# Top-k attention and an MLP-mixer on one core: which score tiles are masked by an adding DMA, the order of the first loads, and a newly fitted instruction order

## The chip, the cores and the metric

The kernel runs on one core of a Trainium2 chip. The metric is the device time of one execution in microseconds (us). Three runs of the kernel before gave 759.48, 761.50 and 761.62 us; the median is 761.5 us.

## The reference

The reference is attention over 8 batches of 8 heads, 576 positions and a head size of 64, in which each row keeps only its 32 largest scores, followed by a token and channel mixing MLP on the joined heads. In short:

```python
scores = scale * q @ k.T                      # (8, 8, 576, 576)
kth    = 32nd largest of each row
attn   = softmax(where(scores >= kth, scores, -1e9))
x      = join_heads(attn @ v)                 # (8, 576, 512)
h      = relu(x.T @ w_tok1) @ w_tok2          # 576 -> 256 -> 576
u      = x + h.T
out    = u + relu(u @ w_ch1) @ w_ch2          # 512 -> 1536 -> 512
```

## The kernel before

The work goes by pairs of heads, 32 pairs in all (`pair_ops(p)`), four pairs to a batch. A pair has five groups of score tiles: groups 0 to 3 hold one tile of 128 rows of each of the two heads, and group 4 is a single tile that holds the last 64 rows of both heads. So a pair has nine tiles of 128 rows by 576 columns, and the kernel has 288.

Each tile passes through all engines in turn. TensorE transposes q and k (L426) and makes the scores in PSUM (`products`, L488, for the groups of two; `last`, L494, for the single tile). ScalarE copies them into an `Sb` buffer (L578). VectorE takes the eight largest of each of seven segments (L588) and narrows the 56 candidates in five dependent steps (L593 to L600); this gives an upper bound for the 32nd largest. GpSimd shifts and scales the scores by that bound into integers (L632). ScalarE counts by the sign how many lie above (L635), GpSimd appends eight dummy values made from the count (L638), and VectorE takes the eight largest of the remaining integers (L643), among which the 32nd largest of the row stands at a known place. GpSimd turns it into a threshold (L651) and writes a byte mask `U` (L666): a row's dropped scores get a huge negative number, the kept ones none.

The masked exponentials are then made in one of two ways:

- **Recomputed.** TensorE puts the mask into PSUM as a product with a scaled identity (`lower`, L510, for a pair of tiles; `again`, L500 and L504, for a single one), adds the scores once more on top of it, and ScalarE takes the exponential from PSUM into a `Pm` buffer (L676 for a pair, L682 for a single tile). There are two `Pm` buffers.
- **Added by DMA.** ScalarE takes the exponential of the unmasked scores early, from `Sb` into a `Pe` buffer (L625). When the mask is there, GpSimd issues a DMA that adds `U` to `Pe` as 16-bit integers (L686). There are four `Pe` buffers. TensorE has no part in it.

The set `ADDED` says which groups (p, g) go the second way. In both ways SyncE then issues a transposing DMA into `PT` (single tiles: `PTl`), L690, TensorE multiplies by v (`pv`, L706), and VectorE divides by the row sums (`norm`, L715 and L716). The last groups of pair 31 go a third way (`direct`, L529 to L564), in which VectorE masks and TensorE transposes.

After the fourth pair of a batch, `mlp_ops(b)` adds the MLP of that batch: L751 to L834 on TensorE, its evictions on ScalarE (L763, L791, L811, L842). The last batch's MLP is cut up (`token`, `channel`): nine of its twelve column blocks are begun with half of the sum (L941, called L964), saved by ScalarE (L966), and finished by an addition on VectorE (L989). A self-check (`judge`, L1074 to L1117, and the flag, L1126 and L1129) runs on VectorE near the end; if it fails, the whole result is recomputed by slower code.

No engine's order is written by hand. `Plan` is a list scheduler that runs while the kernel is built: each operation has an engine, a duration, dependencies, buffers that it takes from pools (`Sb` 11, `Pm` 2, `Pe` 4, `PT` 6, PSUM 4), and a due time made of its tile's number times `T` plus an entry of the table `DUE`. Among the operations that could start at about the same time, the one with the earliest due time goes first. Every engine, and every DMA queue, then works strictly in that order. In idle time of TensorE between two fixed points, the scheduler also puts small filler matmuls (L370), six at a time.

At the start, the first pair's loads are issued by hand-set priorities: k's halves on ScalarE's and SyncE's queues (L455), q in pieces on SyncE's (L449: the first 128 rows of both heads, then the other three blocks; L460: the last 64 rows), k's last rows on ScalarE's (L467). Before that, VectorE builds constants (L313, L314) and clears the unused part of the load buffers (L318).

## Time and profile before

One execution was profiled. Its own time was 763.86 us, and the span from its first to its last instruction 762.1 us; the median of the three runs shown above is 761.5 us.

| what | value |
|---|---|
| profiled execution, its own time | 763.86 us |
| span in the profile | 762.1 us |
| TensorE busy | 728.7 us (96%) |
| VectorE busy | 718.8 us (94%) |
| ScalarE busy | 684.4 us (90%) |
| GpSimd busy | 586.4 us (77%) |
| mean granted TensorE clock | 0.995 |

Engines are named PE (TensorE matmuls), PEld (its weight loads), DVE (VectorE), ACT (ScalarE), POOL (GpSimd) and SP (SyncE); a name with q is that engine's queue of instructions, which waits and issues DMAs. A busy PE is not a PE at its peak, because matmuls overlap and their ends are modelled. In the list of instructions over time a row gives start, duration, engine, line, operation, tiles, shapes and count, and in brackets how long the engine stood idle before it and what ended that.

### The profile page before, as it was taken

To read this page: it belongs to the slowest core of one execution; us is meant where nothing else is said; L and a number is where in the kernel's file an instruction comes from. 1 tells how busy PE (TensorE), PEld (TensorE's weight loads), DVE (VectorE), ACT (ScalarE), POOL (GpSimd) and SP (SyncE) were. 2 spreads that over 40 slices of the span, in tenths; PEclk is the share of its full clock that TensorE was granted. 3 is DMA by queue.
4 is the path that set the end of the run, shared out by engine and by line. 5 is a ranking of instruction groups with operands and counts; after the bars stand their busy time and mean duration, and the time that the engine had idled before them with its cause. 6 is when DMAs were issued, how large, how long until landed. Compare 5 with 4: busy or idle time off the path is not lost.

```text
span 762.1 us, 21660 instructions
## 1 busy us (share of the span) xinstructions
PE 728.7 (96%) x6517; PEld 508.1 (67%) x6517; DVE 718.8 (94%) x4466; ACT 684.4 (90%) x1350; POOL 586.4 (77%) x1053
## 2 busy tenths in 40 slices
PE   6989999999999999999999999999989999999997
PEld 4766777677657776667666765667747776677663
DVE  7997999999999999999999999999999999999861
ACT  5868999899889998999989998899989999999852
POOL 3696989987877878778787878877789888988600
PEclk9998999999999999999999999999999999999999
DMA  5598999967887678767787656887759988876602
GB/s 124 91 157 145 142 158 180 170 124 118 148 147 140 125 115 163 151 119 128 118 157 151 121 108 123 168 162 126 139 115 166 152 135 160 137 125 88 123 18 72
DMA packets 293658, 101.15 MB, mean 133 GB/s; under 512 B 269856, under 2 KB 290208, under 8 KB 293536
## 3 DMA queue, kind: packets, MB, share of 16 engines
q1 hardware_dynamic: 279152, 83.86, 59.0%
q0 software_dynamic: 13632, 15.57, 14.6%
q8 instruction: 52, 0.85, 0.4%
q14 instruction: 70, 0.57, 0.2%
q10 hardware_dynamic: 752, 0.30, 0.1%
HBM read 35.85 MB, written 9.44 MB: 59 GB/s over the span
## 4 chain that ended last, share of the span: by engine, by line
DVE 41%; PE 39%; ACT 8%; POOL 6%; issue 3%; DMA 2%; ACTq 0%; DVEq 0%; POOLq 0%; SPq 0%
DVE cd L588 16%; PE bank L488 13%; DVE tlo L643 12%; PE bank L830 4%; PE bank L805 4%; PE bank L706 3%; ACT sign L635 3%; DVE cd L598 3%; PE bank L510 2%; DVE cd L594 2%; POOL U L666 2%; DVE Xb L716 2%; DVE thi L600 2%; PE bank L494 2%; POOL Sb L632 2%
## 5 line engine op out<-in xcount | busy, mean ns | idle before, releaser
L588 DVE MAX8 cd<-Sb 128x8 f32<-128x82 f32 (+1 forms) x2016 | 386.3, 231 | 2.0 <-ACT Sb L578 1.9
L488 PE MATMUL bank<-kT,qT 64*128 64x288 f32 x1712 | 242.2, 422 | 6.2 <-ACT kT L433 3.8
L635 ACT ACTIVATE sign<-Sb,half 128x576 bf16<-128x576 int32 x283 | 226.9, 802 | 20.4 <-POOL Sb L632 12.9
L666 POOL TENSOR_SCALAR U<-Sb,nt 128x576 uint8<-128x576 int32 x283 | 212.3, 750 | 25.7
L632 POOL TENSOR_SCALAR Sb<-Sb,ng 128x576 int32<-128x576 f32 x283 | 217.2, 779 | 13.2 <-ACT Pe L625 6.0
L643 DVE MAX8 tlo<-Sb 128x8 f32<-128x584 uint32 x283 | 214.0, 756 | 8.8 <-POOL Sb L638 8.0
L488 PEld LDWEIGHTS bank<-kT,qT 64*128 64x128 f32 x1712 | 153.9, 188 | 72.7 <-issue 21.7
L578 ACT COPY Sb<-bank 128x576 f32<-128x576 f32 x288 | 167.5, 685 | 10.3 <-PE bank L488 7.5
L676 ACT ACTIVATE Pm<-bank 128x576 bf16<-128x576 f32 x172 | 105.4, 664 | 7.3 <-PE bank L488 7.1
L805 PE MATMUL bank<-UT,wc1b 128*128 128x288 bf16 x672 | 90.2, 286 | 3.6 <-ACT UT L791 1.5
L830 PE MATMUL bank<-wc2b,H 128*128 128x512 bf16 x372 | 88.1, 379 | 0.4 <-ACT H L811 0.4
L805 PEld LDWEIGHTS <-wc1b 128*128 128x128 bf16 x672 | 64.6, 98 | 27.1 <-issue 9.3
L830 PEld LDWEIGHTS <-H 128*128 128x128 bf16 x372 | 34.6, 98 | 40.8 <-issue 6.0
L635 ACT ACTIVATION_READ_ACCUMULATOR sign<-Sb,half 128x1 f32 x283 | 61.7, 218 | 0.0
L651 POOL TENSOR_SCALAR nt<-tlo 128x2 f32<-128x2 f32 (+1 forms) x157 | 35.8, 228 | 32.3 <-DVE tlo L643 12.8
L510 PE MATMUL bank<-U,identN 128*128 128x288 bf16 x344 | 58.1, 288 | 1.2 <-POOL U L666 0.5
L600 DVE MAX8 thi<-cd 128x8 f32<-128x56 f32 x288 | 58.3, 202 | 0.0
L686 POOL DMA_DIRECT2D Pe<-U x40 | 50.4, 1259 | 6.7 <-POOL U L666 4.5
L811 ACT ACTIVATE H<-bank 128x576 bf16<-128x576 f32 x84 | 54.4, 676 | 0.0
L638 POOL TENSOR_TENSOR Sb<-kdum,cnt 128x16 int32<-128x16 int32 (+1 forms) x157 | 36.7, 235 | 21.5 <-ACT sign L635 17.7
L598 DVE MATCH_REPLACE8 cd<-m,cd 128x35 f32<-128x35 f32 x288 | 52.5, 182 | 0.0
L596 DVE MAX8 m<-cd 128x8 f32<-128x35 f32 x288 | 51.9, 180 | 0.1
(140 smaller groups left out, 1067.9 us busy)
## 6 DMA issues: line engine op xcount, KB each, us to landing
Pe<-U POOLq DMA_DIRECT2D x40, 288.0 KB, 4.7
vL<-in_v_dram SPq DMA_DIRECT2D x32, 256.0 KB, 3.0
kL<-in_k_dram SPq DMA_DIRECT2D x63, 128.0 KB, 3.1
qL<-in_q_dram SPq DMA_DIRECT2D x62, 128.0 KB, 2.9
out_dram<-ob SPq DMA_DIRECT2D x15, 512.0 KB, 3.0
wc1b<-in_moe_w_ch_dram POOLq DMA_DIRECT2D x4, 384.0 KB, 5.1
wc2b<-in_moe_w_ch_dram POOLq DMA_DIRECT2D x4, 384.0 KB, 6.5
PT<-Pm SPq DMA_TRANSPOSE x86, 3.9
```

Source lines behind the costliest of these rows:

```text
L488: nc.tensor.matmul(out=halves(s.t)[:, h, :], lhsT=qT.t[rows(h), g * P : (g + 1) * P], rhs=kT.t[rows(h), i * HS : (i + 1) * HS], start=star ...
L578: ev.append(plan.add("ACT", 0.535, t + DUE["cp"] + 0.01 * i, lambda n=n, i=i, s1=s1, Sb=Sb: nc.scalar.copy(out=Sb.t[:, 0:n, i * HS : (i + ...
L588: ss.append(plan.add("DVE", 0.146, t + DUE["seg"] + 1.0 * h, lambda a=a, h=h, cd=cd, Sb=Sb: nc.vector.max(cd.t[:, a, :], Sb.t[:, h, bounds ...
L598: a4 = plan.add("DVE", 0.157, tr_, lambda m8=m8, cd=cd: nc.vector.match_replace(cd.t[:, :, 0:5], m8.t[:, 1, :], cd.t[:, :, 0:5], NEG), [a3 ...
L600: a5 = plan.add("DVE", 0.12, tr_, lambda i=i, cd=cd: nc.vector.max(thi[:, at(i) - 7 : at(i) + 1], cd.t[:, :, :]), [a4] + tops[-1:], use=[cd])
L632: xo.append(plan.add("POOL", 0.725, t + DUE["x"] + 0.9 * h, lambda k=at(i) - lo, h=h, Sb=Sb, X=X, nb=nb: nc.gpsimd.tensor_scalar(out=X.t[: ...
L635: sgn.append(plan.add("ACT", 0.77, t + DUE["sg"] + 0.8 * h, lambda i=i, h=h, X=X: nc.scalar.activation(out=sign[:, :], in_=X.t[:, h, 0:S]. ...
L643: mxs.append(plan.add("DVE", 0.67, t + DUE["mx"] + 1.2 * h, lambda i=i, h=h, X=X: nc.vector.max(tlo[:, at(i) - 7 : at(i) + 1], X.t[:, h, : ...
L666: us.append(plan.add("POOL", 0.84, t + DUE["u"] + 0.01 * h, lambda h=h, k=at(i0 + h) - lo, nt=nt, U=U, X=X: nc.gpsimd.tensor_scalar(out=by ...
L676: oe.append(plan.add("ACT", 0.54, t + DUE["ex"], lambda i=i, s2=s2, Pm=Pm: nc.scalar.activation(out=Pm.t[:, :, i * HS : (i + 1) * HS], in_ ...
L805: nc.tensor.matmul(out=o[:, i, :], lhsT=wc1b[:, cc, fc * P : (fc + 1) * P], rhs=UT.t[:, cc, i * HS : (i + 1) * HS], start=(cc == 0), stop= ...
L830: nc.tensor.matmul(out=po, lhsT=H2.t[:, fc, cs], rhs=wc2b[:, fc, :], start=(fc == 0), stop=False)
```

## The change

`ADDED` held 40 groups, all of them pairs of tiles: group 1 of pairs 0 to 30 and group 3 of pairs 22 to 30. It now holds 61: group 1 and the single tile, group 4, of pairs 5 to 30, and group 3 of pairs 22 to 30. So 26 single tiles move from recomputing to the adding DMA, and five pairs of tiles (group 1 of pairs 0 to 4) move the other way. On the engines that makes 26 times fewer L500 with L504 and L682 and five times more L510 with L488 and L676; 26 more early exponentials and adding DMAs of one tile, and five fewer of two.

In the first pair, the first 128 rows of q of both heads now come with one DMA, the buffers' unused part is cleared first of all on VectorE, 13 small matmuls (`warm`) go ahead of the first transposes and three behind the first of q, and q's transposes are cut into three pieces (block 0; blocks 1 to 3; the last rows) with a copy for each. Groups 1 to 3 then need only the second piece.

`T` and the whole table `DUE` have new numbers, and a few durations that the scheduler plans with changed by up to 0.04 us. The core of the diff:

```diff
-ADDED = {(p, 1) for p in range(31)} | {(p, 3) for p in range(22, 31)}
+ADDED = {(p, g) for p in range(5, 31) for g in (1, 4)} | {(p, 3) for p in range(22, 31)}
...
-T = 1.71610
+T = 1.64060
 DUE = dict(
...
-    mm=-231.700, mx=-97.622, ng=6.727, nm=1.107, nt=-276.380, pv=-124.790, re=-244.310, rnd=-75.253,
+    mm=-290.100, mx=-210.470, ng=-108.730, nm=-6.943, nt=-334.450, pv=-139.730, re=-276.010,
...
+    for t in qLs + kLs:
+        nc.vector.memset(t[:, 4, :, :], 0.0)
     make_identity(nc, identF[:, :])
...
-    for t in qLs + kLs:
-        nc.vector.memset(t[:, 4, :, :], 0.0)
...
+    def warm(s, n):
+        a = 1024 * s + 1024 - 184
+        for _ in range(n):
+            nc.tensor.matmul(out=bank[:, a : a + 184], lhsT=identB[:, :], rhs=identF[:, :].bitcast(bf16)[:, 0:184],
+                             start=True, stop=True)
...
+            def first_q():
+                nc.sync.dma_start(
+                    out=qL.t[:, 0, :, :],
+                    in_=q[b, h0 : h0 + 2, 0:SM, :].rearrange("h (p t) d -> p t h d", t=4)[:, 0, :, :])
...
+            def turn_first():
+                turn(pq, qL, (0,))()
+                warm(3, 3)
+
+            o0 = plan.add("PE", 0.7, -98.0, turn_first, [q0], acq=[pq, qT], use=[qL], lat=-0.3)
             k1 = plan.add("PE", 0.43, -97.0, turn(pk, kL, (3, 4)), [k0, lc], use=[pk, kT, kL])
-            o1 = plan.add("PE", 0.86, -96.0, turn(pq, qL, (1, 2, 3, 4)), [o0, q1, q2], use=[pq, qT, qL])
+            o1 = plan.add("PE", 0.65, -97.5, turn(pq, qL, (1, 2, 3)), [o0, q1], use=[pq, qT, qL])
+            o2 = plan.add("PE", 0.22, -96.0, turn(pq, qL, (4,)), [o1, q2], use=[pq, qT, qL])
...
-                    [eq[g > 0]] + ek[: i + 1 if n == 2 else 2], acq=[s1[i]] + ([Sb] if i == 0 else []), use=[qT, kT, Sb], mode=3 if n == 2 else 0)
+                    [eq[0 if g == 0 else 1 if g < 4 else 2]] + ek[: i + 1 if n == 2 else 2], acq=[s1[i]] + ([Sb] if i == 0 else []), use=[qT, kT, Sb], mode=3 if n == 2 else 0)
...
+    warm(3, 13)
     for i, o in enumerate(order):
```

Where the new order matters to the steps of the prediction, it reads as follows. Line numbers of the changed kernel are 3 higher around the transposes and 12 higher from the scores on (L488 is now L500, L635 is L647, L676 is L688, L966 is L978).

The first place is TensorE at the very start, in the first pair; `kL_77` and `qL_75` are its load buffers, `qT_85` and `kT_88` the transposed ones. Before:

```order
L426 MATMUL bank<-identF,kL_77 128x128 x3
L426 MATMUL bank<-identF,qL_75 128x128
L426 MATMUL bank<-identF,kL_77 128x128 x2
L488 MATMUL bank<-kT_88,qT_85 128x288 x4
L426 MATMUL bank<-identF,qL_75 128x128 x4
L488 MATMUL bank<-kT_88,qT_85 128x288 x12
L494 MATMUL bank<-kT_88,qT_85 128x288 x2
```

Now, behind thirteen small matmuls, three transposes of k, the first of q and two more of the small matmuls:

```order
L366 LDWEIGHTS identB
L366 MATMUL bank<-identF,identB 128x184
L429 MATMUL bank<-identF,qL_75 128x128 x3
L429 MATMUL bank<-identF,kL_77 128x128 x2
L429 MATMUL bank<-identF,qL_75 128x128
L500 MATMUL bank<-kT_88,qT_85 128x288 x16
L506 MATMUL bank<-kT_88,qT_85 128x288 x2
```

Before, the first four score matmuls stood ahead of the transposes of q's other blocks; now all transposes, that of q's last rows too, stand ahead of the first score matmul.

The second place is ScalarE around the fourth pair's start, where the exponentials of the first pair's groups are taken; `Pm_124` and `Pm_125` are the two `Pm` buffers, and the single tile is the row of 128x576 out of the bank. Before:

```order
L676 ACTIVATE Pm_125<-bank 128x2x288 x2
L578 COPY Sb_93<-bank 128x2x288 x2
L635 ACTIVATE sign,cnt<-Sb_97,half 128x576
L676 ACTIVATE Pm_124<-bank 128x2x288 x2
L578 COPY Sb_94<-bank 128x576
L635 ACTIVATE sign,cnt<-Sb_97,half 128x576
L635 ACTIVATE sign,cnt<-Sb_98,half 128x576 x2
L682 ACTIVATE Pm_125<-bank 128x576
L430 ACTIVATE qT_85<-bank 128x640
L433 COPY kT_88<-bank 128x576
```

Now:

```order
L688 ACTIVATE Pm_124<-bank 128x2x288
L590 COPY Sb_93<-bank 128x2x288 x2
L688 ACTIVATE Pm_124<-bank 128x2x288
L647 ACTIVATE sign,cnt<-Sb_97,half 128x576
L688 ACTIVATE Pm_125<-bank 128x2x288 x2
L590 COPY Sb_94<-bank 128x576
L694 ACTIVATE Pm_124<-bank 128x576
L433 ACTIVATE qT_85<-bank 128x640
L436 COPY kT_88<-bank 128x576
```

The first pair fills `Pm` five times now, where it filled it four times. Between the last exponential into the buffer that the single tile needs and the single tile's own, there stood nine instructions before (three copies, four signs, two exponentials); now there are four (a sign, two exponentials, a copy).

The third place is ScalarE near the end, where the saved halves of the last batch (L966, now L978) and the last masked tiles are copied; `PT` rows are the transposed tiles of the last pair. Before:

```order
L919 CAST UT_142<-bank 128x576
L905 ACTIVATE H_140<-bank 128x2x128
L564 COPY PT_134<-bank 128x640
L676 ACTIVATE Pm_125<-bank 128x2x288 x2
L919 CAST UT_142<-bank 128x576
L564 COPY PT_134<-bank 128x640
L966 COPY Sb_93<-bank 128x576 x2
L966 COPY Sb_91<-bank 128x576 x2
L564 COPY PT_130<-bank 128x640
L676 ACTIVATE Pm_124<-bank 128x2x288 x2
L564 COPY PT_130<-bank 128x640
L966 COPY Sb_96<-bank 128x576 x2
```

Now:

```order
L541 ACTIVATE Sb_97<-Sb_99 128x2x576
L978 COPY Sb_91<-bank 128x576 x2
L978 COPY Sb_94<-bank 128x576 x2
L978 COPY Sb_100<-bank 128x576 x2
L978 COPY Sb_98<-bank 128x576 x2
L550 ACTIVATE sign,cnt<-Sb_99,half 128x576 x2
L688 ACTIVATE Pm_124<-bank 128x2x288 x2
L978 COPY Sb_95<-bank 128x576
L550 ACTIVATE sign,cnt<-Sb_101,half 128x576
L576 COPY PT_135<-bank 128x640 x2
L688 ACTIVATE Pm_125<-bank 128x2x288 x2
L576 COPY PT_131<-bank 128x640 x2
```

The saved halves, and so the matmuls that make them, stood between and behind the copies of the last pair's transposed tiles; now all nine stand ahead of them, the first eight even ahead of the signs of those tiles. On VectorE the self-check (L1074 on), which stood between the last masked tile and the last additions, now stands behind the last addition.

More of the change, by code (lines that the diff above doesn't have):

```diff
@@ L361 @@
             moe_w_ch2[3 * i * P : (3 * i + 3) * P, :].rearrange("(j p) c -> p j c", p=P)))
+    def warm(s, n):
[3 more added lines that the diff above has]
+                             start=True, stop=True)
     def filler(s, k):
-        a = 1024 * s + 1024 - 184
         def f():
             if k is not None:
+                a = 1024 * s + 1024 - 184
                 nc.tensor.matmul(out=bank[:, a : a + 1], lhsT=identF[:, :], rhs=thi[:, k : k + 1], start=True, stop=True)
-            for _ in range(6):
-                nc.tensor.matmul(out=bank[:, a : a + 184], lhsT=identB[:, :], rhs=identF[:, :].bitcast(bf16)[:, 0:184],
-                                 start=True, stop=True)
+            warm(s, 6)
         return f
@@ L790, in mlp_ops @@
             o = plan.add("PE", 0.98, due(0.98), f, [h1] + wl["w2"], acq=[pb] + ([UT] if cc == 0 else []), use=[X, H1, pb])
-            ut.append(plan.add("ACT", 0.54, due(0.0) + 1, lambda cc=cc, pb=pb: nc.scalar.copy(
+            ut.append(plan.add("ACT", 0.58, due(0.0) + 1, lambda cc=cc, pb=pb: nc.scalar.copy(
                 out=UT.t[:, cc, 0:S].rearrange("p (a b) -> p a b", a=2), in_=halves(pb.t)), [o],
```

38 lines of the change are left out of this document (18 added, 20 removed).

## The prediction

> **What bounds the kernel now.** I began with the busy time of each engine by stages, cut where the character of the kernel changes: until the loads of weights end, the long middle, the end of VectorE's searches, the tail. The columns are the length, then busy time of PE, PEld, DVE, ACT and POOL, then clock, DMA share and GB/s.
>
> ```profile
> 8.63:50.00 41.37, 37.82 (x328) 28.97 (x327) 41.09 (x300) 31.43 (x61) 24.97 (x47) 1.00 0.69 124
> 50.00:100.00 50.00, 44.30 (x416) 33.90 (x415) 44.04 (x280) 42.01 (x86) 41.06 (x73) 0.93 0.97 145
> 100.00:600.00 500.00, 488.39 (x4370) 337.78 (x4369) 494.71 (x3132) 474.18 (x942) 411.27 (x743) 1.00 0.77 140
> 600.00:702.80 102.80, 101.49 (x932) 72.33 (x931) 101.34 (x648) 100.99 (x200) 89.98 (x158) 1.00 0.77 127
> 702.80:721.00 18.20, 17.77 (x128) 10.32 (x126) 16.80 (x42) 15.90 (x32) 14.80 (x25) 1.00 0.72 136
> 721.00:762.10 41.10, 34.83 (x344) 22.52 (x341) 16.77 (x41) 17.64 (x32) 0.00 (x0) 0.99 0.19 50
> ```
>
> From 8.6 to 702.8 us VectorE stands still for 0.28 + 5.96 + 5.29 + 1.46 = 13.0 us only, and the change neither adds nor takes an instruction of it. Whatever is taken from TensorE there can be worth 13.0 us at most. After 721 us VectorE is half idle and TensorE carries the chain. Next the waits, to see who made VectorE wait (total, times, longest).
>
> ```profile
> DVE tlo L643 <- POOL Sb L638: 8.0, 10, 4.6
> ...
> DVE rds L715 <- PE bank L706: 6.5, 8, 2.5
> ...
> PE bank L368 <- ACT qT L430: 4.8, 2, 3.9
> ...
> PE bank L488 <- ACT kT L433: 3.8, 5, 1.4
> ...
> ACT Pm L682 <- DMA PT<-Pm: 3.0, 2, 2.7
> ```
>
> One event makes 4.6 of the 8.0. I followed it through the chain of waits and the list over time.
>
> ```profile
> 48.72 7.98 DMA PT<-Pm
> ```
>
> ```profile
> 56.78 0.65 ACT L682 ACTIVATE Pm<-bank 128x576 bf16<-128x576 f32 x1 [2.65 <-DMA PT<-Pm]
> ```
>
> ```profile
> 59.53 4.21 PE L488 MATMUL bank<-kT,qT 64*128 64x288 f32 x16
> ...
> 64.71 2.21 PE L488 MATMUL bank<-kT,qT 64*128 64x288 f32 x16
> ```
>
> ```profile
> 66.49 0.77 DVE L643 MAX8 tlo<-Sb 128x8 f32<-128x584 uint32 x1 [4.62 <-POOL Sb L638]
> ```
>
> A transposing DMA took 7.98 us, where its kind's median is 3.9 (below), while the DMA engines were 97% busy with weights, adding DMAs and loads. ScalarE stood 2.65 us for the `Pm` buffer that it held, the fourth pair's q and k were copied late, TensorE idled 3.9 us, then ran sixteen matmuls in 4.21 us that later took 2.21, and VectorE lost 4.62 us.
>
> **TensorE's work.** In the tail the two ways of masking lie bare on TensorE's queue: a single tile's (L500 to the start of the next line) and a pair's.
>
> ```profile
> 714.54 0.41 PE L500 MATMUL bank<-U,identN 128*128 128x288 bf16 x2
> ...
> 714.78 1.13 PE L504 MATMUL bank<-kT,qT 128*128 128x288 f32 x4
> ...
> 715.75 0.65 PE L898 MATMUL bank<-w2b,H 128*128 128x288 bf16 x4
> ...
> 717.46 0.65 PE L510 MATMUL bank<-U,identN 128*128 128x288 bf16 x4
> ...
> 719.21 0.66 PE L898 MATMUL bank<-w2b,H 128*128 128x288 bf16 x4
> ```
>
> A single costs 715.75 - 714.54 = 1.21 us, a pair 719.21 - 717.46 = 1.75 us. So TensorE loses 26 x 1.21 = 31.5 us and gains 5 x 1.75 = 8.8 us: 22.7 us less. From 100 us on VectorE is the one that is always busy, so nearly all of this turns into idle time of TensorE. What it can bring is in the waits that TensorE caused: the 6.5 us of L715, less two that lie in the tail,
>
> ```profile
> 724.25 0.22 DVE L715 RECIPROCAL rds<-bank 128x10 f32<-128x10 f32 x1 [2.54 <-PE bank L706]
> ...
> 732.43 0.20 DVE L715 RECIPROCAL rds<-bank 128x6 f32<-128x6 f32 x1 [2.15 <-PE bank L706]
> ```
>
> so 1.8 us, and a share of the 3.4 us that L643 has besides its one event. I take **-2 us**; the ends are 0 (nothing but smoothing) and -6.8 (all idle time after 100 us).
>
> **ScalarE and GpSimd.**
>
> ```profile
> L676 ACT ACTIVATE Pm<-bank 128x576 bf16<-128x576 f32 x172 | 105.4, 664 | 7.3 <-PE bank L488 7.1
> ...
> L686 POOL DMA_DIRECT2D Pe<-U x40 | 50.4, 1259 | 6.7 <-POOL U L666 4.5 <-POOL nt L651 1.0 <-POOL ng L609 0.5
> L625 ACT ACTIVATE Pe<-Sb 128x1152 bf16<-128x1152 f32 x40 | 46.8, 1180 | 0.0
> ...
> L682 ACT ACTIVATE Pm<-bank 128x576 bf16<-128x576 f32 x31 | 20.7, 668 | 5.7 <-DMA PT<-Pm 3.0 <-PE bank L504 2.5
> ...
> L336 POOL DMA_DIRECT2D w1b<-in_moe_w_tok_dram x3 | 1.7, 569 | 0.1
> ...
> L529 ACT ACTIVATE Sb<-Sb 128x576 bf16<-128x576 f32 x1 | 0.7, 679 | 0.0
> ```
>
> ScalarE's exponential of one tile is 668 ns from PSUM and 679 from SBUF: 26 x 0.011 = 0.3 us, and the five pairs cost 2 x 664 - 1180 = 148 ns each, 0.7 us; nothing, hidden in its idle time (25.8 us between 100 and 600). GpSimd issues 26 more DMAs of one tile and five fewer of two. The trace has no issue of one tile; the bounds are 569 ns (the small weights) and 1259 ns (two tiles). By the upper, nearer in kind, that is (26 - 5) x 1.26 = 26 us, at least 26 x 0.57 - 6.3 = 8.5. GpSimd has 88.7 us idle between 100 and 600 and behind each issue waits only its own next mask: nothing on the path.
>
> ```profile
> Pe<-U POOLq DMA_DIRECT2D x40, 288.0 KB, 4.7
> ...
> PT<-Pm SPq DMA_TRANSPOSE x86, 3.9
> qL<-in_q_dram SPq DMA_DIRECT2D x64, 16.0 KB, 2.4
> ```
>
> The adding DMA puts up to 4.7 us between a single tile's mask and its transposing DMA, where 1.21 + 0.67 us stood. Single tiles are the pair's last, so `pv` and the norm come some 3 us later. That holds buffers, not VectorE: the norm is due by priority alone, and nothing waits for it until the batch's MLP. SyncE's queue does stand behind such a wait, with the loads of later pairs, which are issued well ahead. Zero, at worst a wait like the 2.65 above now and then.
>
> **The first 100 us.** Without adding DMAs in the first five pairs, five of 288 KB leave the stage in which the DMA engines are 97% busy, so the transposing DMAs land sooner. Against that, all five groups of a pair now go through the two `Pm` buffers, and in the order ScalarE asks for a buffer again after four instructions instead of nine. So the wait of 2.65 us will not vanish, though the masks start earlier too (the first L643 stands nearer to the start). VectorE's 5.96 us of idle time between 50 and 100 bound the gain; I take **-2.5 us**, with ends at -6 and +4 (the event again, nearly as dear, on top).
>
> **The start.**
>
> ```profile
> 3.85 1.18 SPq L460 DMA_DIRECT2D qL<-in_q_dram  x2
> ```
>
> ```profile
> 6.58 2.29 PE L488 MATMUL bank<-kT,qT 64*128 64x288 f32 x8
> ```
>
> ```profile
> 8.63 0.68 DVE L588 MAX8 cd<-Sb 128x8 f32<-128x82 f32 x4 [1.59 <-ACT Sb L578]
> ```
>
> The first scores now wait for q's last rows, issued until 5.03 us, now some 0.6 sooner with one DMA less ahead, and landing 2.4 us after their issue (`qL` in the list of DMAs above): near 6.5 to 6.9, so the first scores come at about 7.1 to 7.5 instead of 6.58. Then they run without the break that the second piece of q made, and the small matmuls may have them start at full speed: here the first eight took 2.29 us, while sixteen took 2.21 at 64.71. [...] The trace shows only that it was slow there, not that sixteen small matmuls cure it. Later first scores and faster following ones cancel: **0**, between -0.8 and +0.8.
>
> **The tail.** It begins with VectorE's last masked tile.
>
> ```profile
> 719.44 1.54 DVE L550 SCALAR_TENSOR_TENSOR Pe<-Sb,nt,Sb 128x576 bf16<-128x576 int32 x2
> ```
>
> ```profile
> 726.03 2.61 PE L941 MATMUL bank<-UT,wc1b 128*128 128x288 bf16 x20
> ...
> 729.52 0.45 PE L556 MATMUL bank<-identB,Pe 128*128 128x128 bf16 x5
> ...
> 731.24 0.78 PE L706 MATMUL bank<-vb,PT 128*128 128x65 bf16 x20
> ```
>
> The last tile is masked at 720.98, but its transposes (L556) run only at 729.52 and the last `pv` at 731.24, since TensorE still has saved halves to make: five groups in the 2.61 us from 726.03, 0.52 us each. In the new order all nine halves stand ahead of the last transposes, so some 8 x 0.5 = 4 us move from behind VectorE's last tile to before it, where TensorE has the time that the dropped masks free. On the other side, the last two-tile group's scores stand behind the seventh batch's MLP now, and VectorE may stand for them by about 1 us. From the last `pv` on the chain is as before. The self-check now follows the last addition; its bulk was run inside VectorE's idle time, and at the end it lies beside TensorE's last ten us and the final landing: zero. I take **-3 us**, between -6 and +2.
>
> **The sum.** -2 - 2.5 + 0 - 3 = -7.5 us. On the profiled execution's own time of 763.86 us that gives 756.4; its span of 762.1 has 1.8 us around it, and it lies 2.4 above the median of the runs, 761.5. On the median the forecast is **754.0 us**.
>
> **The rivals.** (1) *Nothing comes of it.* VectorE's instructions are the same, TensorE's freed time was idle time, and in the tail both engines have as much left as before. For it: 98.9% of the middle is VectorE's; the fit used old durations. Against it: the tail, where VectorE was done 8.5 us before its last tile was fetched. Time 761, from 758 to 763.8. (2) *Slower, by the two `Pm` buffers.* If a buffer's turn (exponential, issue, landing) stays as long as the 7.98 us above, five groups over two buffers ask for 2.5 x (7.98 + 1.3) = 23 us a pair, while VectorE makes a pair in 694.2 / 32 = 21.7; with four groups it was 18.6. It decides from a landing of 21.7 / 2.5 - 1.3 = 7.4 us. Then ScalarE stands in each of pairs 1 to 4, three more events at 4.62 on top of the one known, with no gain in that stage: 754.0 + 2.5 + 3 x 4.62 = 770 us, from 764 to 775. Against it: the DMAs that left. (3) *TensorE goes slow in the middle.* It has a tenth less to do and no fillers there (the last stand early), so its idle time may gather into stretches like the 3.9 us at 54 us, after which sixteen matmuls took 2 us longer. Each such stretch costs 2 us of TensorE; one in each of 26 pairs, half of it passed on, gives 754 + 26 = 780. Against it: the longest wait of TensorE besides that one and the first load's is 1.4 us (L488 for `kT`), and 1.2 us a pair more does not make 3.9. [...]
>
> **How the numbers follow.** The forecast (747 to 758) has 0.62, rival 1 0.19, rival 2 0.15, rival 3 0.04. A measurement of this kernel tells 0.3%, 2.3 us, from no change: 759.2 to 763.8. A quarter of rival 1 lies below, so faster has 0.62 + 0.05 = 0.67, the same 0.14, slower 0.15 + 0.04 = 0.19. The range takes the forecast, rival 1 and the edge of rival 2: 747 to 764 us.
>
> **What would show it.** Right: TensorE's busy time down by some 20 us and VectorE's unchanged; VectorE's idle time between 50 and 100 us below 6 us, with no wait of L643 above 3 us; the last transposes of masked tiles within 3 us of VectorE's last L550, and 37 to 39 us from there to the end. Wrong: a wait of ScalarE for `Pm` in several early pairs (rival 2), L488 in groups of sixteen above 4 us after 100 us (rival 3), or a tail of 41 us behind an unchanged VectorE (rival 1).

## The result and the profile after

The changed kernel is slower. Beside four runs of the kernel before (median 760.49 us) four runs of it gave 765.54 to 771.21 us, median 770.21: ratio 1.0107, 95% interval 1.0080 to 1.0133. On another chip seven more gave 764.05 to 770.41, median 765.72 against 761.31: 1.0064 (1.0040 to 1.0088). By these ratios it costs 0.6 to 1.1%, 5 to 8 us (the medians of the first four lie 9.7 us apart), where 7.5 us of gain were forecast, and its runs scatter more than those of the kernel before.

The first of its runs was profiled (own time 771.21 us, span 769.4). The same stages as before, with the cuts behind 702.8 us at VectorE's last masked tile and at TensorE's last output matmul (length, then PE, PEld, DVE, ACT, POOL busy, clock, DMA share, GB/s):

```profile
8.63:50.00 41.37, 39.07 (x339) 30.75 (x336) 40.98 (x292) 32.27 (x65) 27.68 (x53) 1.00 0.78 127
50.00:100.00 50.00, 44.16 (x414) 31.54 (x412) 46.88 (x306) 42.34 (x90) 41.28 (x75) 1.00 0.87 157
100.00:600.00 500.00, 473.87 (x4223) 325.93 (x4249) 488.16 (x3101) 474.44 (x940) 418.46 (x745) 0.98 0.80 141
600.00:702.80 102.80, 95.47 (x816) 64.45 (x821) 98.15 (x620) 96.20 (x188) 88.99 (x154) 0.97 0.78 133
702.80:732.06 29.26, 24.87 (x250) 16.16 (x250) 23.91 (x83) 27.04 (x53) 24.20 (x40) 1.00 0.63 126
732.06:761.50 29.44, 27.87 (x271) 17.68 (x271) 17.02 (x41) 10.78 (x19) 0.00 (x0) 1.00 0.17 48
```

Read the DVE column against the length. Between 50 and 100 us VectorE is idle for 3.1 us instead of the 6.0 of the profiled execution before (which held a rare event, as the step on the first 100 us shows). From 100 to 702.8 us it is idle for 11.84 + 4.65 = 16.5 us instead of 6.8: 9.7 us are lost where 2 were to be won, and in the same rows TensorE has less to do, its clock is below 1.00 and GpSimd has more to do. Most of the loss is waits of VectorE's second search for GpSimd's dummies. Over the whole span they were 8.0 us before, and 2.9 between 100 and 702.8 us; now the span has 15.9, and that part 11.6.

```profile
DVE tlo L655 <- POOL Sb L650: 15.9, 22, 3.3
```

The busy time of the engines and the clock in 40 slices, from the page:

```profile
PE 711.2 (92%) x6330; PEld 491.5 (64%) x6365; DVE 719.2 (93%) x4466; ACT 686.2 (89%) x1356; POOL 604.9 (79%) x1074
PEclk9999999999999999999989999999979999899998
```

TensorE is down by 17.5 us and VectorE unchanged, as forecast. The clock has three dents in the middle (a shorter one near 117 us does not show in a slice). In the list over time this is the place of the first:

```profile
391.12 0.48 PE L718 MATMUL bank<-vb,PT 128*128 128x65 bf16 x10 [1.48 <-DMA PT<-Pm]
...
394.16 0.73 PE L718 MATMUL bank<-vb,PTl 128*128 128x65 bf16 x10 [2.56 <-DMA PTl<-Pe]
...
395.79 4.18 PE L500 MATMUL bank<-kT,qT 64*128 64x288 f32 x16
...
403.25 0.77 DVE L655 MAX8 tlo<-Sb 128x8 f32<-128x584 uint32 x1 [1.76 <-POOL Sb L650]
```

```profile
392.00:393.00 1.00, 0.00 (x0) 0.00 (x0) 1.00 (x10) 0.91 (x3) 0.82 (x4) 0.99 1.24 235
393.00:394.00 1.00, 0.00 (x0) 0.00 (x0) 0.79 (x3) 0.91 (x3) 0.54 (x1) 0.50 1.49 125
...
400.00:401.00 1.00, 0.95 (x6) 0.51 (x7) 1.00 (x10) 0.98 (x2) 0.71 (x1) 1.00 0.00 0
```

TensorE stood at a product with v, first for a `Pm` tile, then for the single tile that now comes by adding DMA (`PTl<-Pe`). Its clock went to 0.50 for 6.8 us (393.0 to 399.8), sixteen score matmuls took 4.18 us instead of 2.21, and VectorE waited 1.76 us afterwards.

The tail, in order: VectorE's last masked tile, TensorE's last product for the output, the last store's issue, and the drains at the program's end (shortest, median and longest in ns); behind them the drain rows of the kernel before.

```profile
731.24 0.82 DVE L562 SCALAR_TENSOR_TENSOR Pe<-Sb,nt,Sb 128x576 bf16<-128x576 int32 x1
...
761.10 0.39 PE L1017 MATMUL bank<-identB,UT 128*128 128x128 bf16 x4
...
762.13 0.55 ACTq L1065 DMA_DIRECT2D out_dram<-ob  x1
```

```profile
L1337 POOLq DRAIN  x3: 40/107/4447, 764.1 to 769.1; - x3
```

```profile
L1324 POOLq DRAIN  x3: 40/107/3099, 738.3 to 761.8; - x3
```

From the last mask (732.06) to the last output matmul (761.49) it takes 29.4 us instead of 35.7 (720.98 to 756.67): 6 us are won, more than the 4 that the forecast counted. But the mask is 11.1 us late, and the end is 7.9 us behind the last matmul instead of 5.4. There GpSimd's long drain begins at 764.1 us; in the kernel before it began at 738.3. It begins when GpSimd has read the flag of the self-check, and the self-check now stands last (e4 below moves both).

| mark | before, us | after, us | shift |
|---|---|---|---|
| first search of VectorE | 8.63 | 9.02 | +0.4 |
| VectorE's idle time, 50 to 100 us | 5.96 | 3.12 | -2.8 |
| VectorE's idle time, 100 to 702.8 us | 6.75 | 16.49 | +9.7 |
| VectorE's last masked tile | 720.98 | 732.06 | +11.1 |
| TensorE's last output matmul | 756.67 | 761.49 | +4.8 |
| end of the span | 762.1 | 769.4 | +7.3 |

### The profile page after: what moved, and what is told of

It is laid out like the page before. It is cut to its first block, busy times and chain, and to the rows that moved or that the text cites. A ratio compares the mean times of both kernels' runs of the same rounds, so it can differ in the third digit from the quotient of the medians.

```text
span 769.4 us, 21347 instructions
## 1 busy us (share of the span) xinstructions
PE 711.2 (92%) x6330; PEld 491.5 (64%) x6365; DVE 719.2 (93%) x4466; ACT 686.2 (89%) x1356; POOL 604.9 (79%) x1074
## 4 chain that ended last, share of the span: by engine, by line
DVE 43%; PE 28%; POOL 14%; ACT 6%; issue 5%; DMA 1%; SPq 0%; ACTq 0%; POOLq 0%; DVEq 0%
DVE cd L600 17%; DVE tlo L655 13%; PE bank L500 8%; POOL U L678 5%; POOL Sb L644 4%; PE bank L817 3%; DVE cd L610 3%; POOL Pe L698 3%; PE bank L718 3%; PE bank L842 3%; DVE cd L606 2%; DVE Xb L728 2%; PE bank L522 2%; DVE thi L612 2%; ACT sign L647 2%
## 5 line engine op out<-in xcount | busy, mean ns | idle before, releaser
L500 PE MATMUL bank<-kT,qT 64*128 64x288 f32 x1752 | 253.9, 428 | 10.3 <-ACT kT L436 7.3
L647 ACT ACTIVATE sign<-Sb,half 128x576 bf16<-128x576 int32 x283 | 226.3, 800 | 16.8 <-POOL Sb L644 8.3
L655 DVE MAX8 tlo<-Sb 128x8 f32<-128x584 uint32 x283 | 214.2, 757 | 16.6 <-POOL Sb L650 15.9
L500 PEld LDWEIGHTS bank<-kT,qT 64*128 64x128 f32 x1752 | 159.8, 190 | 80.1 <-issue 23.5
L590 ACT COPY Sb<-bank 128x576 f32<-128x576 f32 x288 | 169.9, 673 | 10.5 <-PE bank L500 3.2
L688 ACT ACTIVATE Pm<-bank 128x576 bf16<-128x576 f32 x182 | 112.9, 666 | 10.6 <-PE bank L500 8.6
L842 PE MATMUL bank<-wc2b,H 128*128 128x512 bf16 x348 | 85.6, 379 | 1.5 <-issue 0.3
L698 POOL DMA_DIRECT2D Pe<-U x61 | 68.3, 1119 | 12.1 <-POOL U L678 11.0
L522 PE MATMUL bank<-U,identN 128*128 128x288 bf16 x364 | 65.2, 291 | 11.7 <-POOL U L678 9.3
L647 ACT ACTIVATION_READ_ACCUMULATOR sign<-Sb,half 128x1 f32 x283 | 60.9, 215 | 0.0
L650 POOL TENSOR_TENSOR Sb<-kdum,cnt 128x16 int32<-128x16 int32 (+1 forms) x157 | 41.8, 267 | 24.3 <-ACT sign L647 20.0
L637 ACT ACTIVATE Pe<-Sb 128x1152 bf16<-128x1152 f32 (+1 forms) x61 | 57.5, 961 | 0.7 <-DMA PT<-Pe 0.7
L522 PEld LDWEIGHTS <-identN 128*128 128x128 bf16 x364 | 33.4, 98 | 31.9 <-issue 17.1
```

The costliest lines, as they stand in the source:

```text
L500: nc.tensor.matmul(out=halves(s.t)[:, h, :], lhsT=qT.t[rows(h), g * P : (g + 1) * P], rhs=kT.t[rows(h), i * HS : (i + 1) * HS], start=star ...
L522: nc.tensor.matmul(out=halves(s.t)[:, h, :], lhsT=identN[:, :], rhs=U.t[:, h, i * HS : (i + 1) * HS], start=True, stop=False)
L590: ev.append(plan.add("ACT", 0.535, t + DUE["cp"] + 0.01 * i, lambda n=n, i=i, s1=s1, Sb=Sb: nc.scalar.copy(out=Sb.t[:, 0:n, i * HS : (i + ...
L647: sgn.append(plan.add("ACT", 0.77, t + DUE["sg"] + 0.8 * h, lambda i=i, h=h, X=X: nc.scalar.activation(out=sign[:, :], in_=X.t[:, h, 0:S]. ...
L655: mxs.append(plan.add("DVE", 0.67, t + DUE["mx"] + 1.2 * h, lambda i=i, h=h, X=X: nc.vector.max(tlo[:, at(i) - 7 : at(i) + 1], X.t[:, h, : ...
L688: oe.append(plan.add("ACT", 0.54, t + DUE["ex"], lambda i=i, s2=s2, Pm=Pm: nc.scalar.activation(out=Pm.t[:, :, i * HS : (i + 1) * HS], in_ ...
```

## The experiments

Ratios are to runs of the kernel before on the same chip. Some edits leave a part of the computation out, as their expectations say; they keep the order of all other instructions, so that one load can be taken away by itself.

**TensorE's work, in the old order and in the new.**

```diff
 # e1, kernel before, pairs 5 to 30: the single tile's score matmuls
-            for i in range(2):
+            for i in range(0 if 5 <= p < 31 else 2):
```

> The kernel before, its order of instructions unchanged on every engine, with one thing left out: the four score matmuls of the recomputed single tile in pairs 5 to 30, so that the single tile's exponential sees only its mask (this part of the computation is wrong in it). TensorE loses 26 x 0.8 = 21 us of work (four matmuls in 1.13 us, of which the next line's start covers some 0.3), about what the change takes from it (22.7). Theory A (TensorE, with less to do, stands longer, its granted clock halves, and its slow matmuls then make VectorE wait): mean granted clock from 0.995 down to about 0.98, stretches at 0.5 between 100 and 700 us, time 765 to 770 us. Theory B (the new order makes the waits, the clock only follows): clock stays at 0.99 or above, time 759 to 762 us as before.

758.15 us, 0.9958 (0.9941 to 0.9975), mean clock 0.996 to 1.000. Faster: TensorE's load alone does not bring the loss, and freed time of TensorE is worth some 3 us in the old order. Theory A, as a matter of load, falls.

```diff
 # e2, changed kernel: ahead of a pair's first scores and of its product with v
+            if 5 <= p < 31:
+                idle(O.t, 5)          # five matmuls of 184 columns
```

> The changed kernel with throwaway matmuls and nothing else: five small ones (92 ns each) ahead of the first score matmul of each of pairs 5 to 30 and five ahead of each such pair's product with v, 26 x 10 x 0.092 = 24 us, what the change took away; the order of all else is unchanged. Theory A: fewer stretches at half clock between 100 and 702.8 us, the mean granted clock back to 0.99 or more, VectorE's loss there back from 16.5 us (11.84 + 4.65) toward 6.75 (5.29 + 1.46), time 761 to 764 us. Theory B: the waits stay, TensorE has more to do: 770 to 775 us.

781.65 us, 1.0282 (1.0259 to 1.0305), clock 0.988 to 0.992. The clock rose and the time too. At these places TensorE has no room: 24 us more work cost 13 to 17 us, though the trace shows 33 us of idle time between 100 and 702.8 us.

```diff
 # e3, changed kernel: fillers until 690 us of planned time
-    SINCE, UNTIL, GAP, BLOCK, EVERY = 15.0, 140.0, 0.8, 0.46, 0.62
+    SINCE, UNTIL, GAP, BLOCK, EVERY = 15.0, 690.0, 0.8, 0.46, 0.62
```

> The changed kernel with the scheduler's filler matmuls allowed until 690 instead of 140 us of planned time, so some thirty blocks of six more, only where the plan has TensorE idle for 0.8 us or more; the order of all else is unchanged. Theory A: where the plan's idle time is the real one, the clock stays up: 761 to 767 us and a mean clock of 0.985 or more. Theory B: 769 to 772 us.

764.50 us, 1.0062 (1.0041 to 1.0084), clock 0.992 to 0.997. The fillers do what they are for: no slow stretch is left in the middle (clock 1.00 in every hundred us from 100 to 700), and at the place shown above the same sixteen matmuls take 2.21 us again.

```profile
392.75 0.48 PE L718 MATMUL bank<-vb,PTl 128*128 128x65 bf16 x10 [1.57 <-DMA PTl<-Pe]
393.65 2.21 PE L500 MATMUL bank<-kT,qT 64*128 64x288 f32 x16
```

But the ratio is that of the next kernel (e4), whose clock is 0.981 to 0.992.

**The late flag.**

```diff
 # e4, changed kernel, one entry of the table
-    zj=275.080
+    zj=240.000
```

> The changed kernel with one number of the table: zj 240 instead of 275.08, so that VectorE's self-check stands between its last masked tile and the last additions again, and GpSimd reads the flag some 20 us before the end. Theory C (the end is 2.4 us longer because GpSimd's last drain of 4.45 us begins only when the flag is known): from TensorE's last matmul to the end of the span 5.7 us instead of 7.9, time 2.3 us less than the changed kernel's, 767 to 769 us. Against it (the end is the final store's landing): no change, or 1 us more for the check's instructions ahead of the additions.

765.43 us, 1.0062 (1.0037 to 1.0087). In the trace the end moved as theory C says: GpSimd's long drain begins at 753.9 us,

```profile
L1337 POOLq DRAIN  x3: 40/107/4447, 753.9 to 762.4; - x3
```

and the end of the span (762.6) is 5.5 us behind the last matmul (757.12) instead of 7.9. In the medians 2.4 us cannot be told from the scatter of this kernel.

The changed kernel without an edit (e5), and with both edits, UNTIL 690 and zj 240 (e6):

> The changed kernel once more, unaltered, so that the runs beside it are compared on one chip. Every theory: 768 to 771 us, a mean clock of 0.98, and in its trace whether the stretch at half clock near 115 us, which stood in the first trace and not in that of the kernel with the early flag, comes back (3.4 us of VectorE's time).

765.72 us, 1.0064 (1.0040 to 1.0088). The stretch near 115 us is not in its trace.

> The changed kernel with two of the edits tried before together: filler matmuls allowed until 690 us of planned time, and the self-check between the last masked tile and the last additions (zj 240). If the slow clock and the late flag are two separate costs, they add: 764.5 less 2.1 (the end behind TensorE's last matmul fell from 7.9 to 5.8 us), 761 to 764 us, the same as the kernel before. If the fillers only won what other waits give back, 765 us or more.

764.79 us, 1.0043 (1.0025 to 1.0060), clock 0.994 to 0.998. Beside e5 that is 0.9 us less; the two intervals allow anything from nothing to 4 us. In its trace the end lies 6.8 us behind the last matmul, so that the early flag won 1.1 us there and not 2.4. Clock and flag are real but small: with both mended, the order is still slower than the old one.

**The waits of the last two pairs.** In each trace of the new order so far VectorE waits 4.5 to 4.7 us between 700 and 718 us (in e2, which is later, between 715 and 725). The changed kernel again (e5):

```profile
704.55 0.77 DVE L655 MAX8 tlo<-Sb 128x8 f32<-128x584 uint32 x1 [1.20 <-POOL Sb L650]
...
710.39 1.57 DVE L655 MAX8 tlo<-Sb 128x8 f32<-128x584 uint32 x2 [1.36 <-POOL Sb L650]
713.62 1.56 DVE L600 MAX8 cd<-Sb 128x8 f32<-128x82 f32 x10 [1.66 <-ACT Sb L590]
```

```diff
 # e7, changed kernel: the seventh batch's MLP, last stage
-                        for fc in range(6 * part, 6 * part + 6):
+                        for fc in range(6 * part, 6 * part + (2 if b == 6 else 6)):
```

> The changed kernel with two thirds of the last matmul stage of the seventh batch's MLP left out (4 of 6 matmuls of each half sum, 32 in all, 6.9 us; this part of the output is wrong in it), the order of all else unchanged. It tells what makes VectorE wait 4.7 us between 700 and 718 us (1.19 + 0.32 + 1.36 + 1.65 + 0.17, the same in three traces of this order). Theory T1 (the last groups' scores stand behind that MLP on TensorE): these waits fall to 1.5 or less, time 3 to 4 us below the changed kernel's on the same chip. Theory T2 (they come from GpSimd's and ScalarE's own chain, mask and sign): they stay within 1 us, time within 1 us.

768.65 us, 1.0080 (1.0060 to 1.0100). Theory T1 falls, and more: the first waits stay and the last grows from 1.66 to 2.67 us,

```profile
703.76 0.77 DVE L655 MAX8 tlo<-Sb 128x8 f32<-128x584 uint32 x1 [1.19 <-POOL Sb L650]
...
709.60 1.58 DVE L655 MAX8 tlo<-Sb 128x8 f32<-128x584 uint32 x2 [1.35 <-POOL Sb L650]
713.84 1.56 DVE L600 MAX8 cd<-Sb 128x8 f32<-128x82 f32 x10 [2.67 <-ACT Sb L590]
```

while TensorE, with less to do there, lost its clock (0.50 from 709.4 to 712.8 us):

```profile
705.00:710.00 5.00, 1.82 (x16) 0.94 (x16) 3.33 (x5) 4.34 (x10) 4.73 (x10) 0.94 0.64 102
710.00:715.00 5.00, 4.81 (x29) 3.21 (x29) 2.30 (x10) 4.25 (x9) 4.43 (x8) 0.72 0.55 160
```

**One part alone.** Three kernels took one part of the change over into the kernel before and let the scheduler lay out the order anew.

```diff
 # e8: the set only
-ADDED = {(p, 1) for p in range(31)} | {(p, 3) for p in range(22, 31)}
+ADDED = {(p, g) for p in range(5, 31) for g in (1, 4)} | {(p, 3) for p in range(22, 31)}
 # e11, kernel before: T and the table
-T = 1.71610
+T = 1.64060
 # e12, kernel before: first loads, turns, small matmuls, as in the diff above
+    warm(3, 13)
```

> The kernel before with one line changed: the set of groups on the adding DMA is the new one, and the scheduler lays out the order with the old table and the old first loads. Theory S (the set as such is good or harmless, and what went wrong is the refitted order): 756 to 761 us and a clock of 0.99 or more, as the kernel before with its single tiles' score matmuls left out (758.2). Theory A (single tiles on the adding DMA leave TensorE idle in stretches and hold SyncE's queue, whatever the order): clock 0.985 or less and 765 us or more. Theory F (a table fits only the set that it was fitted for): 765 us or more too, but with many short waits of VectorE at a clock of 0.99 or more.

773.37 us, 1.0170 (1.0146 to 1.0195). Its middle is as good as that of the kernel before (VectorE is busy for 493.96 of the 500 us from 100 on; before: 494.71); it loses in the late pairs (93.74 of 102.8 from 600 on; before: 101.34). Neither S nor A nor F fits the whole of it.

> The kernel before with the new T and table alone, on the old set and the old first loads. If the new table is bad for itself: 766 us or more, with the waits of the last two pairs (4.7 us between 700 and 718) in it. If a table only fits its set, the same, but with losses spread over the whole run. If the set is what costs: 759 to 763 us.

773.72 us, 1.0157 (1.0122 to 1.0192). The new table is bad for the old set. The waits of the last two pairs are not in its trace: VectorE's long waits stand at 111.7, 646.6 and 723.5 us (2.88, 4.27 and 2.53).

> The kernel before with the new first loads, turns and small matmuls alone, on the old set and the old table, so that the scheduler lays the rest out again from a start that it plans otherwise. Its first 50 us tell the start by itself: the first search of VectorE at 9.0 us instead of 8.6, as in the changed kernel, and the first sixteen score matmuls in about 2.2 us instead of 4.5 for the first pair's first groups. Its whole time tells how much a table depends on the start: within 1% of 761, 757 to 769 us; no theory of the first part forbids either side.

782.72 us, 1.0276 (1.0239 to 1.0312). The start itself costs nothing: 32 score matmuls run without a break in 4.15 us, at a granted clock of 1.00, and VectorE begins at 8.56 us (8.63 before).

```profile
7.09 4.15 PE L500 MATMUL bank<-kT,qT 64*128 64x288 f32 x32
...
8.56 1.55 DVE L600 MAX8 cd<-Sb 128x8 f32<-128x82 f32 x10 [1.12 <-ACT Sb L590]
```

All three alone are worse than all together. A table fits one program; whoever changes a part lays out another order, 12 to 21 us slower. What a part is worth can't be had by undoing it. The runs below therefore keep an order and take away a load.

**GpSimd's load.**

```diff
 # e9, changed kernel: no adding DMA for single tiles
+                lambda n=n, U=U, Pm=Pm: None if n == 1 else nc.gpsimd.dma_start(
 # e10, e1's kernel: an adding DMA more behind each single tile's mask
+                    nc.gpsimd.dma_start(out=spare[:, :].bitcast(u16), in_=U.t[:, 0, 0:448], accum_op=ALU.add)
```

> The changed kernel without the 26 single tiles' adding DMAs (the single tiles of pairs 5 to 30 then keep unmasked exponentials; this part of the computation is wrong in it); the order of all else is unchanged. GpSimd loses 26 x 0.96 = 25 us of issues ((68.3 - 35 x 1.24) / 26), and SyncE's transposing DMAs of the single tiles no longer stand for a landing. Theory G (the added issues and landings made VectorE's new waits, of which the same order shows about nine in every trace: 1.7 at 399, 0.7 at 516, 0.7 at 567 and 590, 1.4 at 639, 1.9 at 658, then 1.2, 1.4 and 1.7 from 704 to 714 us): most of them go, time 4 to 7 us below the changed kernel's 766 to 770, 760 to 764 us. Theory P (they stand in the order itself, who is due when on ScalarE, TensorE and VectorE): they stay, 765 to 769 us.

765.12 us, 1.0045 (1.0024 to 1.0066). A gain of 0.2% on e5, too small to tell, and its trace shows no more: most of the waits stay, and the end lies 5.8 us behind the last output matmul instead of 7.9, since GpSimd's drain, with 26 adding DMAs fewer, takes 2.69 us instead of 4.45. So 25 us less on GpSimd (580.3 us busy) bought nothing ahead of the end that these runs can tell. P seemed right.

> The kernel before with the single tiles' score matmuls left out as in the first experiment, and on top of it 26 adding DMAs issued by GpSimd right behind the single tiles' masks (448 of 576 columns, into a spare buffer that nobody reads); its order is otherwise the old one. It pairs with the one before: the new load on GpSimd and the DMA queues in the old order. Theory G: VectorE's waits appear here too, 763 us or more. Theory P: 757.5 to 760 us, as without the DMAs (758.15).

778.15 us, 1.0218 (1.0184 to 1.0252): 20 us more than e1, 0.77 us for each of 26 issues that take 0.93 us of GpSimd and keep it waiting 0.32 us for their mask. ScalarE and VectorE wait for GpSimd; e10 first, then e1:

```profile
ACT sign L637 <- POOL Sb L634: 29.9, 30, 2.9
DVE tlo L645 <- POOL Sb L640: 20.8, 28, 1.9
```

```profile
ACT sign L635 <- POOL Sb L632: 16.1, 17, 1.9
...
DVE tlo L643 <- POOL Sb L638: 3.4, 11, 0.9
```

So P fails here: an issue that the plan does not know costs nearly its whole length, at a GpSimd that is idle for a fifth of the span. GpSimd's waits for the landings are not behind it: there is one, of 1.6 us. It does not tell what a planned one costs. For that one load after another was taken from the new order.

```diff
 # e13, changed kernel: early exponentials read another buffer
-                out=Pm.t[:, 0:n, 0:S], in_=Sb.t[:, 0:n, 0:S], func=AF.Exp, scale=scale / SHRINK), evs[g], acq=[Pm], use=[Sb, Pm])]
+                out=Pm.t[:, 0:n, 0:S], in_=w2b[:, 0:n, :], func=AF.Exp, scale=scale), evs[g], acq=[Pm], use=[Sb, Pm])]
 # e14, changed kernel: no adding DMA
+                lambda n=n, U=U, Pm=Pm: None and nc.gpsimd.dma_start(
 # e15, changed kernel: second halves of the recomputed pairs' exponentials
+                lambda i=i, s2=s2, Pm=Pm: None if i and p >= 5 else nc.scalar.activation(
 # e16, changed kernel: second score matmuls of the recomputed pairs
+                None if p >= 5 else products(g, s2[i], i, False)
```

> The changed kernel with its 61 early exponentials at their places in ScalarE's queue, but reading a weight buffer instead of the scores (their values are wrong in it), so that GpSimd's scaling, which overwrites the scores in place, no longer waits for them. Theory X (the scaling stands behind a late early exponential: for the tile of the wait at 399 us the bound was ready at 384.3, the exponential ran at 391.7 to 392.9 and the scaling at 393.0): the waits at 399, 567, 590 and 704, whose tiles go that way, shrink by half or more, time 2 to 5 us below the changed kernel (1.0064 of the kernel before): 0.999 to 1.004. Theory Q (each queue is simply full at these places): the waits stay, 1.004 to 1.008.

766.17 us, 1.0068 (1.0046 to 1.0090). Theory X falls.

> The changed kernel without any of its 61 adding DMAs (the tiles that go that way stay unmasked, wrong in it), the order of all else unchanged: GpSimd has 68 us less to do. If GpSimd's load is the cause, the wait at 639 us (a single tile whose scaling stood behind GpSimd's work without a gap from 631.8 on) and those at 516, 704 and 710 go: 0.996 to 1.001 of the kernel before. If not: 1.003 to 1.007, as without the 26 single ones (1.0045).

757.98 us, 0.9962 (0.9949 to 0.9974): 1.0% below the changed kernel. VectorE's waits for GpSimd's dummies fall from 13.2 us (e5) to 7.1,

```profile
DVE tlo L655 <- POOL Sb L650: 13.2, 23, 1.7
```

```profile
DVE tlo L655 <- POOL Sb L650: 7.1, 10, 1.4
```

the two at 516 and 590 us go and that at 399 falls to 0.33; that at 639, which was to go, stays (1.25 at 632), and so do the four between 694 and 703 us (1.19, 0.41, 1.35, 2.19). The clock rose with it (0.989 to 0.992; e5: 0.981 to 0.991). And a part of the 1.0% is not a load on the queue at all: without adding DMAs GpSimd's drain takes 1.06 us instead of 4.45, so the late flag costs nothing.

```profile
748.17 0.39 PE L1017 MATMUL bank<-identB,UT 128*128 128x128 bf16 x4
```

```profile
L1337 POOLq DRAIN  x3: 40/107/1057, 750.4 to 753.8; - x3
```

The span ends at 754.1, 5.5 us behind the last output matmul instead of 7.9: 2.4 of the 7.8 us, 0.3%, are the end's.

> The changed kernel with the second half of the exponential left out for every recomputed pair of tiles from pair 5 on (those columns are wrong in it), the order of all else unchanged: ScalarE has some 78 x 0.67 = 52 us less to do (a half of 156 exponentials). If ScalarE's load is the cause: signs and early exponentials come sooner, most of the nine waits go, 0.994 to 1.001 of the kernel before. If not: 1.003 to 1.008.

765.52 us, 1.0068 (1.0040 to 1.0095). ScalarE's load is not it.

> The changed kernel with the second score matmuls left out for every recomputed pair of tiles from pair 5 on (those exponentials see only their mask, wrong in it), the order of all else unchanged: TensorE has about 312 x 0.14 = 43 us less to do. If TensorE's load is the cause of the waits: 0.994 to 1.001 of the kernel before, if its clock holds. If a less busy TensorE only loses its clock more often: a mean clock of 0.97 or less and 1.006 or more.

762.64 us, 1.0032 (1.0012 to 1.0052), clock 0.974 in the profile (e5: 0.984). TensorE's load gives a third of what the adding DMAs give, though the clock fell.

```diff
 # e17, changed kernel: in place of each adding DMA
+        for c in (448, 448) if n == 2 else (448, 200):
+            nc.gpsimd.tensor_scalar(out=spare[:, 0:c], in0=w2b[:, 0, 0:c], scalar1=1.0, scalar2=None, op0=ALU.mult)
 # e18, kernel before: no adding DMA
+                lambda n=n, U=U, Pm=Pm: None and nc.gpsimd.dma_start(
```

> The changed kernel without its 61 adding DMAs (those tiles stay unmasked, wrong in it), and at the place of each two small GpSimd instructions on a spare buffer that take about as long as the issue did (about 1.2 us for a pair of tiles, 0.9 for a single), the order of all else unchanged. If GpSimd's time is what costs: back to 1.003 to 1.008 of the kernel before, with the waits at 399, 516 and 590 us. If the landing and the transposing DMAs behind it are what costs: 0.995 to 0.999, as without the issues (0.9962).

825.15 us, 1.0840 (1.0818 to 1.0861). The size was missed: an instruction took 1.33 us, not 0.6, so that GpSimd was busy for 677.7 us (e14: 535.8; changed kernel: 604.9). It answers the question all the same: without any adding DMA, 142 us of GpSimd's time cost 67 us, and VectorE's waits for it are 69.6 us.

```profile
DVE tlo L661 <- POOL Sb L656: 69.6, 59, 3.5
```

Time of GpSimd alone is enough; whether the landings cost something besides stays open.

> The kernel before without its 40 adding DMAs (those tiles stay unmasked, wrong in it), its order unchanged: 50 us of GpSimd's time less. If the price is one that both kernels pay by the issue (1% for 61): 0.992 to 0.996, and the new load costs the difference of 21 issues, 0.3%. If the old order had room for its issues and the new one has not: 0.997 to 1.001.

756.05 us, 0.9945 (0.9927 to 0.9964). The kernel before pays 0.55% for its 40 issues, the changed one 1.0% for its 61 (1.0064 to 0.9962). But of the 1.0% the end of the span has 0.3, as shown for e14, while here the end stays 5.4 us behind the last matmul, with the DMAs and without. On the queue that leaves 0.55% for 40 and 0.7% for 61, no more by the issue. (By the first four runs, at 1.0107, it would be 1.1%.) Without the adding DMAs the two orders stand 0.2% apart.

## Why the prediction was wrong, step by step

- **ScalarE and GpSimd: "nothing on the path". This step failed.** The price of GpSimd's issues was set to zero because GpSimd has idle time and "behind each issue waits only its own next mask". What stands behind an issue on GpSimd's queue are also the scaling and the dummies of other tiles, which VectorE's second search waits for. That GpSimd's time lies on the path is shown by e18 (the old order pays 0.55%, 4 us, for its 40 issues), e10 (20 us for 26 issues more) and e17 (67 us for 142). What the change itself added here is not as clear. GpSimd's busy time rose by 18.5 us (586.4 to 604.9). All issues cost 0.55% before and 0.7% now on the queue: 1 us more by e5, with an interval that reaches down to nothing, and 4 to 5 by the first four runs, the profiled one of which holds the event told under rival 2. A further 2.4 us is the drain at the end, named under the tail. "GpSimd becomes the bound behind VectorE" was not among the rivals.
- **TensorE's work, -2 us. By size this term missed most.** The reason was sound in the old order (e1: -3 us for 21 us less work), but in the middle 9.7 us were lost in the profiled execution, 6.6 in e5's. The term took TensorE's freed time as something that can only shorten VectorE's waits, and put the order that comes with it at nothing. In that order VectorE's waits for the dummies grow, and the adding DMAs are what they hang on most (from 100 us to the last pairs, one trace each; e14's was the fastest of its runs):

| kernel | waits for the dummies, us |
|---|---|
| before | 2.9 |
| before, no adding DMA (e18) | 1.5 |
| changed, first trace | 11.6 |
| changed again (e5) | 8.9 |
| no adding DMA of a single tile (e9) | 7.2 |
| less work of TensorE (e16) | 6.2 |
| clock held (e3) | 4.9 |
| no adding DMA at all (e14) | 3.1 |

- **Rival 3, 0.04.** It did happen, at five places of the profiled execution between 100 and 700 us, and the point from which it decides was taken wrong: the longest waits of TensorE ahead of them were 1.10 to 2.77 us, not 3.9 (last section). The L500 groups of sixteen above 4 us after 100 us were the sign named for it. Its price was far too high: with the clock held (e3, e6) no more than some 4 us come back, not 26.
- **The first 100 us, -2.5, and the start, 0.** Against the profiled execution of the kernel before they came out right: 2.8 us less idle time in the stage, 0.4 us later a start, no wait of VectorE's second search above 3 us there. But the number was luck, and the step that took the term from that execution was wrong: the event of 4.62 us on which it rests is rare. The edits of e1 and e10 begin with pair 5, so both share the old order here, and neither has it. The row is e1's:

```profile
50.00:100.00 50.00, 45.86 (x444) 35.19 (x440) 48.86 (x304) 46.03 (x95) 45.06 (x81) 1.00 1.01 157
```

VectorE is idle for 1.14 us, in e10 as well, and not for 5.96; by them the new order loses 2 us in this stage. Of the 85 runs of the kernel before that stood beside the experiments nine have a mean clock of 0.995 or less, as that execution had, and take 762.5 to 766.7 us; all others but one stay below 762.5. So a forecast for the median had nothing to win from this event. The start's 0.4 us are within its scatter: 8.57 to 9.30 in the traces of the new start, 8.22 to 8.63 in the old.

- **Rival 2, 0.15.** It fell as a rule for pairs 1 to 4. Its mechanism stands at pair 4 in some of the runs:

```profile
115.30 1.19 ACT L688 ACTIVATE Pm<-bank 128x576 bf16<-128x576 f32 x2 [1.79 <-DVE cd L600]
...
121.28 0.65 ACT L694 ACTIVATE Pm<-bank 128x576 bf16<-128x576 f32 x1 [3.14 <-issue]
...
124.90 0.77 DVE L655 MAX8 tlo<-Sb 128x8 f32<-128x584 uint32 x1 [3.30 <-POOL Sb L650]
```

A transposing DMA issued at 106.3 us landed only after 8.9 us, at 115.2 (in e5 after 4.2). Until then ScalarE stood for its `Pm` buffer, though the row names a VectorE event just behind the landing. TensorE stood for ScalarE, 2.8 us, and its clock went to 0.50 from 116.5 to 119.9; the single tile's product came late, ScalarE stood for that, and VectorE lost 3.3 us. The event is in the traces of the changed kernel, e13, e15 and e17, where this DMA took 8.9 to 9.2 us, and not in those of e2 to e7, e9, e14 and e16, which share this early part, where it took 4.1 to 6.8: rival 2's bound was 7.4. Of the kernels that add no work, the three that have it show the highest own times (769.9 to 771.2 us), which suggests that it makes a good part of the scatter.

- **The tail, -3.** Its own term was right and small: 6 us were won behind the last mask. Two others were mis-sized. VectorE's waits for the last groups were put at "about 1 us" and are 4.7, against 0.9 before; the reason given, the scores behind the MLP, is refuted by e7. And the late self-check was set to zero, with "it lies beside TensorE's last ten us": the flag itself releases GpSimd's long drain, 2.4 us (e4, e14).

The sum of the terms in the profiled execution: +0.4 - 2.8 + 9.7 = +7.3 us at 702.8 us; +3.8 of waits until the last mask; -6.3 from there to the last matmul; +2.5 at the end. That is +7.3, the difference of the two spans. It is the sum for two single executions, the first of which held the early event.

The signs that were named for "right" came all the same: TensorE's busy time down by 17.5 us with VectorE's unchanged, less than 6 us of idle time between 50 and 100 us without a wait above 3, and the last transposes 1.5 us behind the last mask, with 37.3 us from there to the end.

```profile
732.54 1.00 PE L568 MATMUL bank<-identB,Pe 128*128 128x128 bf16 x15
```

None of them looked at VectorE's idle time from 100 to 702.8 us, where the loss stood.

**What stays open.** The four waits between 694 and 718 us survive every load that was taken away (e7, e9, e13 to e16). The last pairs leave VectorE little else to do, so that the chain of scaling, sign and dummies may lie bare; that is argued, not shown. Why the middle of the new order waits more is shown only in part. It hangs on the adding DMAs (e14), but not on the 26 single tiles by themselves (e9 moved 0.2%, and the end of the span alone has as much), and by the issue the new order pays no clearly higher price than the old one. That its order leaves less room at GpSimd for any issue is argued, not shown; e14 also lets TensorE keep more of its clock, and that share was not measured by itself.

## What to carry to other kernels

An engine that is 80% busy and stands three or four times in every tile's chain is not idle: price a new instruction there by what is queued behind it, and test it by taking the load away with the order kept. Where a scheduler's table was fitted, parts of a change can't be told apart by undoing them; leave out work, never re-plan, and see how much of a gain is only a shorter end of the program. A cost that shows in one profiled execution may be a rare event: look for it in a second one before forecasting its loss as a gain. When an order moves a check to the end, look at what its result releases.

## What the runs showed of the hardware

- The granted clock fell without a pause of 3.9 us ahead of it. In the profiled execution of the changed kernel it stands at 0.50 in five stretches between 100 and 700 us: from 116.5 to 119.9, 393.0 to 399.8, 560.2 to 567.1, 573.9 to 577.3 and 652.4 to 659.2. The longest waits of TensorE that began in the 5 us ahead of these were 2.77, 2.56, 1.90, 1.10 and 2.10 us, in this order. A wait of 1.79 us, from 359.99 to 361.78, had no such stretch behind it: 1.00 until 365.7. What decides it was not shown.
- GpSimd's last drain took 4.45 us in the programs with 61 adding DMAs, 3.10 with 40, 2.69 with 35 (e9) and 1.06 without (e14, e17, e18). In e10, with 40 and 26 shorter ones, it took 0.98, so the count alone does not set it.
- GpSimd's issue of an adding DMA takes 0.89 to 0.94 us for one tile of the changed kernel and 1.22 to 1.29 for two: twice the data costs a third more, so single tiles are dear by this way.
- A multiplication of 448 columns of bf16 into bf16 took GpSimd 1.33 us (e17), where 576 columns from 32-bit into 32-bit or bytes take 0.75 to 0.82.
